# Layer 2 of chunks 8 to 23 by Strassen's seven products, with p multiplied into x ahead of layer 1

## Chip, cores and metric

One core of one Trainium2 chip. The metric is the device time of one execution, in microseconds (us), as a median over several runs. Every run that a comparison uses is fast (granted TensorE clock 0.994 to 1.0). The rounds ran on several chips, so kernels are compared by their ratio to the kernel before in the same rounds.

## The reference, cut

An RWKV-5 recurrence over 4 batches, 8 heads, 768 steps and 48 columns per head gives x (3072 rows of 384). A mixture of four dense experts, weighted by p, follows. This second part is where the change works:

```python
p = domain_probs / (domain_probs.sum(-1, keepdims=True) + 1e-09)
out = np.zeros((N, D))                    # N, D, E, F = 3072, 384, 4, 1024
for e in range(E):
    h = np.maximum(x @ w1[e], 0.0)        # layer 1
    out += p[:, e:e + 1] * (h @ w2[e])    # layer 2
```

## The kernel before: what the argument touches

The kernel works on 24 chunks of 128 rows; four chunks (one of each batch) make a superchunk, so there are six superchunks, 0 to 5. All matmuls are bf16. The attention of a chunk makes x; layer 1 takes a whole superchunk (512 columns), layer 2 one chunk at a time (8 matmuls of 384 columns for an expert), and p goes in as the layer-2 result leaves PSUM:

```python
def mm(ci=ci, s=s, i=None):                       # layer 2, one chunk, one expert
    ...
    for fb in range(NFB) ...:                     # NFB = 8
        nc.tensor.matmul(ps, tl["hTs", e, sc][:, fb, s, :], w2_sb[:, e, fb, :],
                         start=(fb == 0), stop=(fb == NFB - 1))

def evac(ci=ci):
    ...
    if e == 0:
        nc.scalar.mul(tl["oacc", ci], tl["o", e, ci], pe)
    else:
        nc.vector.scalar_tensor_tensor(tl["oacc", ci], in0=tl["o", e, ci], scalar=pe,
                                       in1=tl["oacc", ci], op0=ALU.mult, op1=ALU.add)
```

Attention gives VectorE, per chunk, two scales (RK), two masks (AtM), a row reduction (dcoef), one addition (Ysb) and the state update (Tn), and GpSimd the products ruk, dv and the other half of the state:

```python
eng.tensor_mul(RK[:, i, :, 0:D], tl[("Kt", "Rt")[1 - i], ci],
               tl["W", i] if ci < SUB and i not in on_pool else W_sd[i])      # scale, two inputs in SBUF
...
nc.gpsimd.tensor_mul(tl["ruk", ci], tl["Rt", ci], tl["Kt", ci])
...
nc.vector.tensor_mul(tl["AtM", ci][:, j], tl["At", ci, j], mask[...])         # the mask; At is in PSUM
...
nc.vector.tensor_add(tl["Ysb", ci]..., tl["Y", ci], tl["dv", ci])             # Ysb; Y is in PSUM
```

The order of instructions on each engine isn't written by hand. Every piece of work is a `job` with the engines that may do it and a duration in us, such as `{"V": 0.61}` for a mask on VectorE or `{"P": 0.98}` for ruk on GpSimd. When the program is built, a small planner plays these durations through and fixes the order and, where there is a choice, the engine. A wrong duration doesn't give a wrong result; it gives an order that doesn't fit. At run time each engine takes its instructions strictly in that order.

## Time and profile before

| | before |
|---|---|
| time, median of 3 runs (lowest to highest) | 295.73 us (294.98 to 295.81) |
| profiled span | 293.9 us |
| busy: PE, PEld, DVE, ACT, POOL | 287.9, 170.0, 159.4, 150.5, 105.5 us |

PE is TensorE's matmul, PEld its weight load (beside PE), DVE is VectorE, ACT ScalarE, POOL GpSimd. A window of the profile lists, for one stretch of the span, the busy time of each engine; 25.00 of 25.00 for PE means that TensorE had no gap. The prediction below shows the lines that matter; two further windows of the kernel before (columns: stretch, length, then PE, PEld, DVE, ACT, POOL busy with counts, granted clock, share of the transfer engines, GB/s):

```profile
75.00:100.00 25.00, 24.99 (x238) 15.74 (x236) 18.41 (x32) 12.12 (x21) 19.64 (x25) 1.00 0.79 152
150.00:175.00 25.00, 25.00 (x175) 13.76 (x174) 12.07 (x22) 12.39 (x22) 11.09 (x14) 1.00 0.61 131
```

TensorE is full, and VectorE is at 18.4 of 25 us early, at 12.1 later.

### The profile page before, as it was taken

How to read it: one execution, taken by the hardware profiler on the slowest of the kernel's cores; microseconds unless marked ns; L12 is line 12 of the kernel's file. 1: busy time of each engine (PE TensorE's matmuls, PEld its weight loads, DVE VectorE, ACT ScalarE, POOL GpSimd, SP SyncE). 2: the span in 40 equal slices, each digit the busy share in tenths (PEclk: the TensorE clock that was granted, in tenths of full speed). 3: DMA queues.
4: the chain of work that ended last, by engine and by line, in shares of the span. 5: the costliest groups of instructions: out<-in, count | busy, mean ns of one | idle time of the engine just before them, and what ended most of it. 6: DMA issues, size and time to landing. Idle time of an engine off the chain costs nothing.

```text
span 293.9 us, 5824 instructions
## 1 busy us (share of the span) xinstructions
PE 287.9 (98%) x2298; PEld 170.0 (58%) x2298; DVE 159.4 (54%) x300; ACT 150.5 (51%) x249; POOL 105.5 (36%) x138
## 2 busy tenths in 40 slices
PE   8989999999999999999999999999999999999995
PEld 3777566866855555555555555555555555555553
DVE  6877877786579895727537535546405222101223
ACT  4573968557843334464444464543564544565440
POOL 2885144844977583754522542411000000000000
PEclk9999999999999999999999999999999999999999
DMA  7999999999966769592192391130330100200003
GB/s 153 257 266 284 308 322 283 214 312 186 229 122 125 164 143 200 152 187 41 22 205 55 103 202 34 28 71 29 107 74 6 20 2 27 80 2 0 0 2 107
DMA packets 111199, 37.66 MB, mean 128 GB/s; under 512 B 99242, under 2 KB 111148, under 8 KB 111172
## 3 DMA queue, kind: packets, MB, share of 16 engines
q1 hardware_dynamic: 111156, 37.29, 53.7%
q8 instruction: 18, 0.29, 0.4%
q14 instruction: 9, 0.07, 0.1%
q10 hardware_dynamic: 16, 0.00, 0.0%
HBM read 26.79 MB, written 4.72 MB: 107 GB/s over the span
## 4 chain that ended last, share of the span: by engine, by line
PE 90%; SPq 6%; DMA 2%; POOL 0%; issue 0%; DVE 0%
PE out_ps L632 42%; PE hT_ps L602 37%; PE hT_ps L596 4%; SPq L191 4%; DMA wst<-in_moe_w_dram 2%; PE At_ps L436 2%; PE Y_ps L474 1%; SPq L205 1%; PE Y_ps L467 1%; PE St_ps L515 1%; SPq L202 1%; PE RKT_ps L394 1%; PE out_ps L565 0%; POOL w_sb L76 0%; PE xT_ps L500 0%
## 5 line engine op out<-in xcount | busy, mean ns | idle before, releaser
L613 ACT ACTIVATE hTs<-hT_ps 128x512 bf16<-128x512 f32 x168 | 99.8, 598 | 99.2 <-PE hT_ps L602 94.4
L632 PE MATMUL out_ps<-w_sb,hTs 128*128 128x384 bf16 x760 | 137.9, 326 | 0.1
L602 PE MATMUL hT_ps<-xTe,w_sb 128*128 128x512 bf16 x504 | 123.7, 379 | 0.0
L632 PEld LDWEIGHTS <-hTs 128*128 128x128 bf16 x760 | 72.9, 98 | 53.0 <-issue 0.2
L642 DVE SCALAR_TENSOR_TENSOR oacc<-out_ps,p_nat,oacc 128x384 f32<-128x384 f32 x71 | 43.6, 617 | 90.7 <-PE out_ps L632 89.5
L602 PEld LDWEIGHTS <-w_sb 128*128 128x128 bf16 x504 | 47.0, 98 | 46.4
L345 POOL TENSOR_TENSOR ruk<-Rt,Kt 128x384 f32<-128x384 f32 x24 | 23.9, 1000 | 43.3 <-DMA Kt<-in_k_dram 25.0
L445 DVE TENSOR_TENSOR AtM<-At_ps,mask 128x512 bf16<-128x512 f32 x48 | 30.7, 683 | 14.0 <-PE At_ps L436 14.0
L371 POOL TENSOR_TENSOR dv<-Vt,dcoef 128x384 f32<-128x384 f32 x24 | 21.3, 888 | 32.5 <-DVE Ysb L483 28.7
L353 POOL TENSOR_TENSOR ruk<-ruk,U_sd 128x384 f32<-128x384 f32 x23 | 24.7, 1075 | 0.9
L640 ACT ACTIVATE oacc<-out_ps,p_nat 128x384 f32<-128x384 f32 x24 | 13.8, 581 | 18.8 <-PE out_ps L632 14.7
L535 POOL TENSOR_TENSOR S<-Tn,wC 64x192 bf16<-64x192 f32 x32 | 17.3, 542 | 6.5 <-DVE Tn L530 5.0
L596 PE MATMUL hT_ps<-xTe,w_sb 128*128 128x128 bf16 x288 | 18.0, 219 | 0.9 <-ACT w_sb L72 0.7
L366 DVE TENSOR_REDUCE dcoef<-ruk 128x8 f32<-128x384 f32 x24 | 13.1, 545 | 10.7 <-POOL ruk L353 10.3
L76 POOL CAST Vb<-Vt 128x384 bf16<-128x384 f32 x20 | 12.4, 618 | 14.7 <-PE St_ps L515 6.8
L596 PEld LDWEIGHTS <-w_sb 128*128 128x128 bf16 x288 | 16.6, 98 | 1.5 <-ACT w_sb L72 0.9
L483 DVE TENSOR_TENSOR Ysb<-Y_ps,dv 128x384 bf16<-128x384 f32 x24 | 13.3, 553 | 6.6 <-PE Y_ps L474 5.2
L611 ACT ACTIVATE hTs<-hT_ps 128x512 bf16<-128x512 f32 x24 | 14.2, 597 | 4.3 <-PE hT_ps L596 3.3
L332 DVE TENSOR_TENSOR RK<-Kt,W_sd 128x384 bf16<-128x384 f32 x20 | 16.2, 814 | 0.0
L332 DVE TENSOR_TENSOR RK<-Rt,W_sd 128x384 bf16<-128x384 f32 x20 | 14.6, 734 | 0.2
L72 ACT CAST w_sb<-wst 128x768 bf16<-128x768 f32 (+1 forms) x12 | 11.9, 990 | 3.4 <-DMA wst<-in_moe_w_dram 3.3
L530 DVE TENSOR_TENSOR Tn<-S,St_ps 64x192 f32<-64x192 bf16 x32 | 11.1, 348 | 1.6 <-PE St_ps L515 0.9
(67 smaller groups left out, 138.1 us busy)
## 6 DMA issues: line engine op xcount, KB each, us to landing
wst<-in_moe_w_dram SPq DMA_DIRECT2D x16, 576.0 KB, 6.2
Kt<-in_k_dram SPq DMA_DIRECT2D x24, 192.0 KB, 3.9
Vt<-in_v_dram SPq DMA_DIRECT2D x24, 192.0 KB, 4.3
Rt<-in_r_dram SPq DMA_DIRECT2D x24, 192.0 KB, 3.7
out_dram<-oacc SPq DMA_DIRECT2D x23, 192.0 KB, 1.9
wst<-in_moe_w_dram SPq DMA_DIRECT2D x8, 384.0 KB, 6.7
RKT<-RK SPq DMA_TRANSPOSE x16, 3.2
xTe<-Ysb SPq DMA_TRANSPOSE x16, 2.3
```

The source lines that it names most:

```text
L332: eng.tensor_mul(RK[:, i, :, 0:D], tl[("Kt", "Rt")[1 - i], ci], tl["W", i] if ci < SUB and i not in on_pool else W_sd[i])
L345: nc.gpsimd.tensor_mul(tl["ruk", ci], tl["Rt", ci], tl["Kt", ci])
L353: nc.gpsimd.tensor_mul(tl["ruk", ci], tl["ruk", ci], U_sd)
L371: nc.gpsimd.tensor_mul(tl["dv", ci], tl["Vt", ci], tl["dcoef", ci].to_broadcast((128, H, D)))
L445: nc.vector.tensor_mul(tl["AtM", ci][:, j], tl["At", ci, j], mask[:, None, :].to_broadcast((128, NP, C)))
L535: nc.gpsimd.tensor_mul(S_new[pr, :, cl], tl["Tn", ci][pr], wC[pr, :, None].to_broadcast((P2, NP, D)))
L596: nc.tensor.matmul(ps[:, i, :], w1_sb[:, e, db, (fb + i) * 128:(fb + i + 1) * 128], xTe[:, db, s0, :], start=(i == 0 and db == 0), stop=(i ...
L602: nc.tensor.matmul(ps[:, 0:n, :].rearrange("p a b -> p (a b)"), w1_sb[:, e, db, fb * 128:(fb + 1) * 128], xTe[:, db, s0:s0 + n, :].rearran ...
L611: nc.scalar.activation(hTs[:, fb:fb + 4, s0, :], ps, AF.Relu)
L613: nc.scalar.activation(hTs[:, fb, s0:s0 + n, :], ps[:, 0:n, :], AF.Relu)
L632: nc.tensor.matmul(ps, tl["hTs", e, sc][:, fb, s, :], w2_sb[:, e, fb, :], start=(fb == 0), stop=(fb == NFB - 1))
L642: nc.vector.scalar_tensor_tensor(tl["oacc", ci], in0=tl["o", e, ci], scalar=pe, in1=tl["oacc", ci], op0=ALU.mult, op1=ALU.add)
```

## The change

Strassen's scheme forms a 2x2 block product from seven products instead of eight. Here the two row blocks are two chunks, the two column blocks halves of w2's 384 columns, and the inner blocks even and odd groups of the hidden dimension. Seven eighths of the matmul work of layer 2 remain, for additions on other engines. So that one scheme can run over all four experts as one long sum of products, p must already be inside the hidden values: x is multiplied by p (p is positive, so ReLU lets it through), once for each expert, before layer 1. The change does this for superchunks 2 to 5 (chunks 8 to 23). What each part costs:

- 20 weight mixes (sums of w2 blocks), once, on VectorE or GpSimd: `mix`;
- four scalings by p for each chunk, on ScalarE or VectorE, into one buffer `y_e`, which one transposing transfer of 12 blocks empties: `xs`;
- ten sums of hidden blocks for each pair of chunks, on VectorE: `sum`;
- seven products of 16 matmuls of 192 columns for each pair, and their combination into the output.

For room, buffers become fixed shared regions, some of them fewer (three input buffers for four, two of Ysb, ruk and dv for three). `GATES` says after which layer-1 group the attention of each pair of chunks may begin.

```diff
-    NIN = 4
+    NIN = 3
...
+    w2_t = weights.tile([128, 3, E, NFB // 2, Dm // 2], BF16)
+    hAll = weights.tile([128, E * NFB, SUB, 128], BF16)
+    NST = 12
+    stg = weights.tile([128, NST, 2 * Dm], F32)
...
+    GATES = (3, 3, 4, 2, 8, 10, 13, 19)
...
-    slots = dict(inp=NIN, wst=8, RKT=4, AtM=2, Ysb=3, ruk=3, dv=3, Vb=4, At=2, tr=1, ys=1,
-                 mm=4, xTe=3, hTs=3, oacc=12)
+    FIRST = 2                                        # first superchunk by Strassen
+    slots = dict(inp=NIN, RKT=3, AtM=2, Ysb=2, ruk=2, dv=2, Vb=4, At=2, tr=1, ys=1,
+                 mm=4, xTe=2, oacc=4, Yse=1)
...
+            def xs(e):
+                def run(eng):
+                    o = y_e[:, e * HD:(e + 1) * HD]
+                    if eng == "A":
+                        nc.scalar.mul(o, tl["Ysb", ci], p_nat[:, e, n_p:n_p + 1])
+                    else:
+                        nc.vector.tensor_scalar(o, tl["Ysb", ci], scalar1=p_nat[:, e, n_p:n_p + 1],
+                                                scalar2=None, op0=ALU.mult)
+                return run
+            for e in range(E):
+                job(("Xs", ci, e), {"A": 0.48, "V": 0.40}, xs(e), ...)
+            job(("Xout", ci), {"S": 1.3}, lambda: nc.sync.dma_start_transpose(
+                get_xTe(sc)[:, :, ci % B, :], y_e), ...)
...
+        def run(eng):                                # mix
+            (nc.vector if eng == "V" else nc.gpsimd).tensor_tensor(o, x, y, op=op)
+        job(("mix", e, what), {"V": 0.47, "P": 2.0}, run, needs, 14.0 + 0.1 * e)
...
+                    job(("sum", sc, q, m, hf), {"V": 0.62},
+                        lambda ...: nc.vector.tensor_tensor(S, a_of(*x, hf), a_of(*y, hf), op=op), ...)
...
+                    for n in range(8):               # one half of one product
+                        ...
+                        nc.tensor.matmul(tl["P", sc, q, m], st, moving(m, e, i),
+                                         start=(hf == 0 and n == 0), stop=(hf == 1 and n == 7))
```

The last chunk of before was split in two to shorten the end; the change drops that.

## The prediction

> **What bounds the kernel now.** I read the page first (busy shares, then the slices), then the sums by window, the chain, the groups, and last the timeline of the end and of one crowded stretch on VectorE and GpSimd.
>
> ```profile
> PE 287.9 (98%) x2298; PEld 170.0 (58%) x2298; DVE 159.4 (54%) x300; ACT 150.5 (51%) x249; POOL 105.5 (36%) x138
> ...
> PEclk9999999999999999999999999999999999999999
> ```
> ```profile
> 50.00:75.00 25.00, 25.00 (x283) 18.04 (x281) 19.53 (x33) 15.88 (x24) 14.92 (x18) 1.00 1.01 236
> 100.00:125.00 25.00, 25.00 (x201) 14.14 (x199) 18.95 (x35) 10.76 (x19) 15.35 (x20) 1.00 0.74 172
> 250.00:275.00 25.00, 25.00 (x137) 13.20 (x135) 3.45 (x6) 13.58 (x23) 0.00 (x0) 1.00 0.07 24
> ```
> The columns of the windows are length, then busy time of PE, PEld, DVE, ACT, POOL. From 25 us to the last store PE has no gap, at full clock. A busy matmul is not by itself a matmul at peak, so I check the pace:
> ```profile
> L632 PE MATMUL out_ps<-w_sb,hTs 128*128 128x384 bf16 x760 | 137.9, 326 | 0.1
> 252.49 1.30 PE out_ps L632 x8
> ...
> 253.79 1.94 PE hT_ps L602 x9
> ...
> 289.48 1.33 PE out_ps L565 x16
> ```
> The 326 ns is one matmul's latency; the chain gives the pace: 1.30/8 = 162.5 ns for 384 columns, 1.94/9 = 216 ns for 512, 1.33/16 = 83.1 ns for 192. So 760 + 504 matmuls of layers 2 and 1 are worth 123.5 + 108.9 us, the 288 small ones of layer 1 some 16 us (48 in 2.68 us), and the remaining 40 us or so are attention, its transposes, fillers and the wait at the start. The chain puts 42% of the span on L632 and 37% on L602. TensorE's amount of work is the bound; the first 25 us hang on loads, the last 3 us on an eviction and a store. VectorE is free on average but not early: 76% in 100 to 125 us, 14% in 250 to 275.
>
> **What the Trainium skill says.**
> 1. "TensorE: Matmul & The Clock Gate", Single matmul latency / Back-to-back issue gap: the isolated gap is N/2.4 + 2.5 ns, so 82.5 ns at 192 columns and 162.5 at 384. The trace agrees (83.1 and 162.5). The same section speaks of about 81 ns at N=128 where weights are reloaded each time; this trace does 55.8 ns there, so the measurement decides: weight loads don't bind at 83 ns.
> 2. "VectorE: DVE Perf Modes", Side-by-side: where the cycles go for N=2048 bf16: a 16-bit two-input add in SBUF runs two elements a cycle at most. The trace before has no such add; it shows two a cycle for a 16-bit copy (424 ns for 512 elements) and one a cycle for the f32 multiplies.
> 3. "SBUF — State Buffer", Who interferes with whom: a VectorE instruction with two SBUF inputs contends with a GpSimd one that reads SBUF, through an exclusive lock. The trace agrees: the scale multiply of K (L332) has minimum 545, median 856, maximum 1387 ns, and is long where GpSimd works:
> ```profile
> 88.20 1.35 DVE L332 TENSOR_TENSOR RK<-Kt,W_sd 128x384 bf16<-128x384 f32 x1
> ...
> 90.39 0.54 DVE L332 TENSOR_TENSOR RK<-Rt,W_sd 128x384 bf16<-128x384 f32 x1
> ```
> ```profile
> 87.81 1.32 POOL L353 TENSOR_TENSOR ruk<-ruk,U_sd 128x384 f32<-128x384 f32 x1
> ```
>
> **The change, part by part.**
> *TensorE.* Layer 2 of 16 chunks is now 504 matmuls of 384 columns and 16 of 192: 504 x 162.5 + 16 x 83.1 = 83.2 us. The instruction order of the changed kernel has 896 of 192 columns (8 pairs, 7 products, 16 matmuls): 896 x 83.1 = 74.5 us. Saved: 8.8 us; the ideal eighth (10.4) loses 1.6 to the fixed cost per matmul. Layer 1 stays at 504 + 288, attention is the same. The start has 96 fillers for 89: seven more at 56 to 110 ns, about +0.5 us of start.
>
> *Moved.* Layers 1 and 2 of a superchunk (four chunks) no longer mix: the order has 96 layer-1 matmuls (20.7 us), then 224 products (18.6 us), with attention between (0.82 us a chunk in the chain: 0.17 + 0.20 + 0.17 and half of a pair's 0.55; 3.3 us per superchunk): 42.6 us.
>
> *ScalarE.* In the pure layer-1 stretch one ReLU comes every 3 x 216 = 648 ns; back to back it takes 0.50 us (two in 1.10):
> ```profile
> 70.00 1.10 ACT L613 ACTIVATE hTs<-hT_ps 128x512 bf16<-128x512 f32 x2
> ```
> 32 x 0.50 = 16 of 20.7 us leave 4.7 us in each superchunk for the scalings by p that the order gives it (29 in all, about 7 x 0.5 = 3.6 us per superchunk). It fits, with four PSUM buffers.
>
> *VectorE.* Removed: 47 weighted accumulations of 617 ns, 29 us. Added: 80 sums of 128x1024 bf16, at two a cycle and the ~140 cycles that the 681 ns masks show over 512: (512 + 140)/0.96 = 0.68 us (estimate), 54 us; 48 combinations of 192 columns at (192 + 142)/0.96 = 0.35 us, 17 us; 8 wide ones at 0.55, 4; 35 scalings by p at about 0.4, 14; 11 weight mixes at about 0.55, 6. Net about +66 us: 159 becomes 225 busy. Successive instructions overlap by about 0.08 us (four masks in 2.48 us, not 2.72), which sets real capacity.
> One product group (two chunks): 10 x 0.60 + 6 x 0.27 + 0.47 = 8.1 us paced, 9.4 by durations, beside 112 x 83.1 = 9.3 us of PE. So pure product stretches (superchunks 4, 5) just go, with attention gone.
> Superchunks 2 and 3 carry attention too: 4 x 4.1 us paced (per chunk two scales 1.55, two masks 1.37, dcoef 0.55, Ysb 0.55, two Tn 0.70, less eight overlaps), p about 3.3, sums and combinations 16.2: 35.9 of 42.6 us, 84%. But scales average 0.77 for 0.545 alone, +0.23 from the lock; if the 20 sums and some 9 p scalings suffer likewise, +6.7: 42.6 us, 100%. This is the tight place.
>
> *GpSimd.* 9 mixes of about 2 us (twice 128x384's 1.0): +18 us before superchunk 2, in stretches where it is up to 79% busy. It also lengthens VectorE's locked time.
>
> *DMA.* Transposes of x carry four times the bytes. From 3 blocks in 2.3 us and 8 in 3.2, about 3.9 us for 12; with a single source buffer about 6 us a chunk, 24 of 43 us. Hidden. Weights come in 32 pieces for 24, same bytes.
>
> *Sum.* 295.7 - 8.8 + 0.5 = 287.4 with no new wait. I add 1.6: 0.2 us per product group (8) for sums arriving late through four buffers; each has 2.0 us (three halves of 8 matmuls) from the release of its buffer until use, of which two semaphore hops and the sum take some 1.1. **289.0 us.** I don't add the 100% in full, since the PE order already interleaves products with other pairs' where sums would be late.
>
> **The rivals.**
> 1. *Clean gain.* VectorE keeps up, nothing is lost: 286.5 to 287.5. For: before, this static order kept PE without a gap for 250 us with VectorE at 76%. Against: only 13% headroom within a product group, where sums form a chain with four buffers.
> 2. *VectorE with GpSimd's lock becomes the bound in superchunks 2 and 3.* PE takes its instructions in order, so a late mask or sum stops it: 3 to 4 us lost in each, 293 to 296, the gain nearly gone. For: the 100% above, and the extra 18 us of GpSimd. Against: superchunk 4's layer 1 has VectorE nearly empty, and PE order has no attention crowding in 4 and 5.
> 3. *The start or weights.* Three input buffers for four, with DMA at 1.01 in 50 to 75 us: late weights open gaps before 100 us, +1 to 3 us: 288 to 291. For: prefetch is shorter. Against: same bytes, and nearly the same loading order up to expert 1.
> 4. *The sums run one element a cycle* because each strides over blocks: 1.2 us each, product groups of 13 us against 9.3: about 315. Inner runs of 128 are contiguous, so I give it 3%.
>
> **Range and chances.** The 2% line is 289.8, only 0.8 above my number: up to 2.4 us of new waits still count as faster. Rival 1 and half of my own central case fall below it; rival 2 and part of 3 above. Faster 0.55, same 0.41, slower 0.04. Range 286.5 to 293.5: clean at the low end, most of rival 2 at the high one.
>
> **What would show it.** Matmul count 896 of 192 columns at 83 ns (1.33 us per 16) in the chain: the saving. PE busy 25.00 in all windows after 25 us: rival 1. Waits of PE's weight loads on VectorE's sums, of 0.1 to 0.3 us, about a product group each: my case. VectorE over 23 of 25 us in the middle windows, sums averaging 0.9 us there and 0.68 in the last two superchunks, and PE waiting for masks or sums by microseconds: rival 2. PE waits for casts before 100 us: rival 3. I am wrong in substance if new PE waits exceed 5 us or if time goes up.

## The result, and the profile after

| | before | after |
|---|---|---|
| time, median of 4 runs (lowest to highest) | 295.77 us (294.98 to 296.91) | 300.04 us (298.18 to 300.81) |
| profiled span | 293.9 us | 298.0 us |
| PE, DVE, ACT, POOL busy | 287.9, 159.4, 150.5, 105.5 us | 281.4, 230.0, 163.1, 125.9 us |

The ratio is 1.0131, with a 95% interval of 1.0092 to 1.0170: slower by 1.3%, within the 2% band, and above the predicted range. A ratio here comes from the fast runs of a kernel and of the kernel before in the same rounds, as the record gives it; it isn't quite the ratio of the quoted medians. Where I compare runs of different rounds below, I turn the ratio into us by (ratio - 1) x 295.7; the change is then +3.9 us.

The page of the changed kernel, busy times and slices (each digit a tenth of a slice of 7.45 us):

```profile
PE 281.4 (94%) x2660; PEld 192.3 (65%) x2681; DVE 230.0 (77%) x430; ACT 163.1 (55%) x285; POOL 125.9 (42%) x147
...
PE   8889999999979969999889999999999999999995
...
DVE  5877689899798999996999998979951179210685
```

PE fell from 98 to 94% of a longer span: TensorE has less to do and stands longer. Between the start and the last slice, the digits below 9 on PE lie in slices 12, 15, 20 and 21, which is about 82 to 156 us, and there VectorE stands at 9. (21 of the 2681 matmuls have no record, up to 2 us of apparent gaps.) The same in windows, columns as above:

```profile
50.00:75.00 25.00, 24.35 (x309) 18.43 (x306) 23.20 (x39) 15.35 (x25) 17.77 (x20) 1.00 0.95 241
75.00:100.00 25.00, 22.68 (x197) 13.32 (x198) 22.56 (x37) 13.49 (x23) 22.16 (x25) 1.00 0.97 170
100.00:125.00 25.00, 22.09 (x183) 12.69 (x185) 24.21 (x42) 9.92 (x18) 18.68 (x22) 1.00 0.90 167
125.00:150.00 25.00, 23.41 (x174) 11.67 (x176) 22.03 (x39) 18.48 (x34) 15.22 (x19) 1.00 1.05 202
150.00:175.00 25.00, 23.28 (x272) 20.32 (x271) 24.84 (x47) 7.45 (x15) 11.24 (x12) 1.00 0.78 149
225.00:250.00 25.00, 24.95 (x214) 18.52 (x215) 11.34 (x22) 13.61 (x24) 0.00 (x0) 1.00 0.08 23
```

From 50 to 175 us VectorE (third busy number) is at 22 to 25 of 25 us, where before it was at 12 to 19.5, and PE loses 0.7 to 2.9 us in each window. From 225 us on, with GpSimd at zero, PE is nearly full again.

The chain of work that ended last (start, duration, what) says what the gaps wait for. Stretches at 107, 134 and 160 us, and the product stretches of superchunks 4 and 5:

```profile
106.92 2.71 DVE stg L530 x3
109.63 0.48 DVE Ysb L514
110.11 0.04 issue
110.15 0.33 PE St_ps L562 x4
...
133.81 6.16 DMA stg<-stg
...
140.06 2.03 DVE stg L530 x3
142.09 0.48 DVE Ysb L514
142.57 0.04 issue
142.61 0.33 PE St_ps L562 x4
...
159.57 3.02 DVE stg L765 x4
...
237.01 18.61 PE M_ps L782 x224
...
276.34 18.62 PE M_ps L782 x224
```

L530 is the scaling by p on VectorE, L514 the Ysb of another chunk behind it in VectorE's order, L562 the state matmul of TensorE that can't begin until Y, which Ysb reads, has left PSUM. So three scalings, 2.71 us, hold up TensorE at 107 us; at 134 us a transposing transfer of the scaled x holds the scalings up first; at 160 us it's sums (L765). From 143 to 178 us the chain runs almost wholly on VectorE. In superchunks 4 and 5, by contrast, 224 products take 18.61 us: 83.1 ns each, without a gap.

The groups that the change added (busy us, mean ns of one, idle time before and its releaser):

```profile
L765 DVE TENSOR_TENSOR stg<-hAll 128x1024 bf16<-128x1024 bf16 x80 | 56.4, 737 | 41.3 <-ACT hAll L648 36.3
L530 DVE TENSOR_SCALAR stg<-Ysb,p_nat 128x384 bf16<-128x384 f32 x35 | 22.4, 686 | 1.9 <-DMA stg<-stg 1.7
L721 POOL TENSOR_TENSOR w_t<-w_sb 128x768 bf16<-128x768 bf16 x5 | 9.2, 1850 | 2.2 <-ACT w_sb L79 1.6 <-DVE w_sb L81 0.6
L721 DVE TENSOR_TENSOR w_t<-w_sb 128x768 bf16<-128x768 bf16 x7 | 7.4, 1073 | 1.4 <-POOL w_sb L83 1.2
L797 DVE TENSOR_TENSOR oacc<-oacc,M_ps 128x192 f32<-128x192 f32 x48 | 15.4, 348 | 1.8 <-PE M_ps L782 1.5
```

Sums average 737 ns (median 685, minimum 678), scalings 686 ns (406 to 1790), mixes on VectorE 1073. Such a spread for instructions of one size is what an instruction looks like that waits inside itself. The timeline (start, duration) of VectorE and then of GpSimd shows it happening:

```profile
102.22 1.34 DVE L362 TENSOR_TENSOR RK<-Rt,W_sd 128x384 bf16<-128x384 f32 x1
103.48 1.99 DVE L362 TENSOR_TENSOR RK<-Kt,W_sd 128x384 bf16<-128x384 f32 x1
```
```profile
102.15 1.00 POOL L375 TENSOR_TENSOR ruk<-Rt,Kt 128x384 f32<-128x384 f32 x1 [1.24 <-DMA Kt<-in_k_dram]
103.11 1.95 POOL L721 TENSOR_TENSOR w_sb<-w_sb 128x768 bf16<-128x768 bf16 x1
```

The scale alone takes 0.545 us. Behind GpSimd's ruk it takes 1.34 us, and behind a weight mix 1.99: it ends at 105.47, 0.41 us after the mix's end at 105.06. VectorE counts as busy all that time.

This holds throughout the trace. Of VectorE's scales, mixes, sums and scalings, 52 take over 50 ns longer than undisturbed, and every one ends a fixed time after the end of a GpSimd instruction: 0.41 to 0.42 us for scales and mixes, 0.55 for sums, 0.21 to 0.22 for scalings. So the scaling, with only one tensor as input, waits too. Counted as mean less minimum, times the number, this waiting fills 29 us of VectorE's time in the change (scalings 9.8, scales 9.5, mixes 5.3, sums 4.7), and 9 us, all in scales, before it.

**The arithmetic.** The matmul saving of 8.8 us and +3.9 us of time leave 12.7 us of lost time, where the prediction had 2.1: 1.6 of new waits and 0.5 at the start.

### The profile page after: what moved, and what is told of

It reads as the page before. It is cut to its first block, busy times and chain, and to the rows that moved or that the text cites. A ratio compares the mean times of both kernels' runs of the same rounds, so it can differ in the third digit from the quotient of the medians.

```text
span 298.0 us, 6749 instructions
## 1 busy us (share of the span) xinstructions
PE 281.4 (94%) x2660; PEld 192.3 (65%) x2681; DVE 230.0 (77%) x430; ACT 163.1 (55%) x285; POOL 125.9 (42%) x147
## 4 chain that ended last, share of the span: by engine, by line
PE 47%; DVE 12%; DMA 2%; issue 2%; DVEq 0%
PE hT_ps L637 23%; PE M_ps L782 19%; DVE stg L765 4%; PE out_ps L666 3%; DVE stg L530 2%; DMA stg<-stg 2%; DVE AtM L475 1%; DVE oacc L797 1%; DVE RK L362 1%; DVE Ysb L514 1%; PE At_ps L466 1%; DVE Tn L577 1%; PE St_ps L562 1%; PE Y_ps L504 0%; PE Y_ps L497 0%
## 5 line engine op out<-in xcount | busy, mean ns | idle before, releaser
L648 ACT ACTIVATE hAll<-hT_ps 128x512 bf16<-128x512 f32 x168 | 97.6, 598 | 43.1 <-PE hT_ps L637 34.7
L765 DVE TENSOR_TENSOR stg<-hAll 128x1024 bf16<-128x1024 bf16 x80 | 56.4, 737 | 41.3 <-ACT hAll L648 36.3
L637 PE MATMUL hT_ps<-stg,w_sb 128*128 128x512 bf16 x372 | 85.5, 379 | 0.6
L782 PEld LDWEIGHTS <-stg 128*128 128x128 bf16 x640 | 52.4, 98 | 2.3 <-DVE stg L765 1.9
L666 PE MATMUL out_ps<-w_sb,hAll 128*128 128x384 bf16 x256 | 46.7, 326 | 0.5 <-POOL w_sb L83 0.5
L782 PE MATMUL M_ps<-w_t,stg 128*128 128x192 bf16 x384 | 36.2, 246 | 0.4 <-DVE stg L765 0.4
L666 PEld LDWEIGHTS <-hAll 128*128 128x128 bf16 x256 | 23.8, 98 | 15.9 <-issue 0.9
L637 PE MATMUL hT_ps<-xTe,w_sb 128*128 128x512 bf16 x111 | 29.2, 379 | 0.6 <-DVE oacc L675 0.2
L782 PE MATMUL M_ps<-w_sb,stg 128*128 128x192 bf16 x256 | 24.4, 246 | 0.2 <-DVE stg L765 0.2
L530 DVE TENSOR_SCALAR stg<-Ysb,p_nat 128x384 bf16<-128x384 f32 x35 | 22.4, 686 | 1.9 <-DMA stg<-stg 1.7
L782 PE MATMUL M_ps<-w_sb,hAll 128*128 128x192 bf16 x256 | 23.1, 246 | 0.0
L782 PEld LDWEIGHTS <-hAll 128*128 128x128 bf16 x256 | 21.2, 98 | 0.6
L646 ACT ACTIVATE hAll<-hT_ps 128x512 bf16<-128x512 f32 x24 | 14.3, 601 | 8.0 <-PE hT_ps L631 7.4
```

The lines of the kernel that those rows point to most:

```text
L530: nc.vector.tensor_scalar(o, tl["Ysb", ci], scalar1=p_nat[:, e, n_p:n_p + 1], scalar2=None, op0=ALU.mult)
L637: nc.tensor.matmul(ps[:, 0:n, :].rearrange("p a b -> p (a b)"), w1_sb[:, e, db, fb * 128:(fb + 1) * 128], xTe[:, x0 + db, s0:s0 + n, :].re ...
L648: nc.scalar.activation(hTs[:, fb, s0:s0 + n, :], ps[:, 0:n, :], AF.Relu)
L666: nc.tensor.matmul(ps, relu_tile(e, sc)[:, fb, s, :], w2_sb[:, e, fb, :], start=(fb == 0), stop=(fb == NFB - 1))
L765: lambda S=S, x=x, y=y, op=op, hf=hf: nc.vector.tensor_tensor(S, a_of(*x, hf), a_of(*y, hf), op=op),
L782: nc.tensor.matmul(tl["P", sc, q, m], st, moving(m, e, i), start=(hf == 0 and n == 0), stop=(hf == 1 and n == 7))
```

## The experiments

The theory, called A in the expectations: new work on VectorE and on GpSimd makes VectorE late, partly because some instructions of the two exclude each other, and TensorE stands behind VectorE. A1 and A2 are two forms of its GpSimd part: exclusion by an instruction that reads, or merely the time that it takes in GpSimd's own queue. The rivals, under other letters or in words, lay the loss on what shorter VectorE and GpSimd instructions would not remove: fewer buffers, transfers, the weights, or the order as such.

All results in one table, fast runs alone. "us" is (ratio - 1) x 295.7.

| run | what it is | median us | ratio (95%) | us against before |
|---|---|---|---|---|
| the change | | 300.04 | 1.0131 (1.0092 to 1.0170) | +3.9 |
| e1_poolmix_short | GpSimd mixes a quarter as wide | 294.22 | 0.9976 (0.9917 to 1.0035) | -0.7 |
| e2_xs_short | VectorE scalings an eighth as wide | 295.45 | 1.0000 (0.996 to 1.004) | 0.0 |
| e3_sums_short | sums of superchunks 2, 3 an eighth as wide | 295.74 | 0.9993 (0.9966 to 1.0019) | -0.2 |
| e4_all_short | all three, and VectorE's mixes | 289.18 | 0.9769 (0.9740 to 0.9797) | -6.8 |
| e5_poolmix_memset | e1, GpSimd's time refilled by writes | 293.66 | 0.9943 (0.9923 to 0.9963) | -1.7 |
| f6_buffers_only | the change with no Strassen superchunk | 299.49 | 1.0138 (1.0113 to 1.0163) | +4.1 |
| g6_no_mixes | f6 without its mixes | 296.39 | 1.0028 (1.0014 to 1.0043) | +0.8 |
| f4_half | Strassen in superchunks 4, 5 | 294.88 | 0.9976 (0.9958 to 0.9994) | -0.7 |
| f3_after_order | Strassen in superchunks 3 to 5 | 294.07 | 0.9937 (0.9909 to 0.9964) | -1.9 |
| g3_early_gates | f3 with the change's early gates | 293.96 | 0.9915 (0.9883 to 0.9947) | -2.5 |
| g2_later_gates | the change with later gates | 297.98 | 1.0060 (1.0036 to 1.0084) | +1.8 |
| h1_two_sources | the change with two `y_e` buffers | 298.19 | 1.0054 (1.0024 to 1.0084) | +1.6 |
| b3_lock_aware | superchunks 3 to 5, order that knows the lock | 289.08 | 0.9782 (0.9768 to 0.9796) | -6.4 |
| b2_lock_aware_all | superchunks 2 to 5, order that knows the lock | 289.71 | 0.9813 (0.9782 to 0.9845) | -5.5 |

e1 to e5 keep every engine's instruction order and only shorten or refill instructions; their results are wrong. So that nothing reads an unwritten buffer, e1, e3, e4 and e5 also give the products other operands of the same size, and e2 and e4 add one memset of 1.38 us on GpSimd; the cuts below leave this out. All the others are correct.

**e1_poolmix_short.** The nine mixes on GpSimd touch a quarter of their columns.

```diff
-            (nc.vector if eng == "V" else nc.gpsimd).tensor_tensor(o, x, y, op=op)
+            n = 1 if eng == "P" else 4
+            (...).tensor_tensor(o[:, 0:n], x[:, 0:n], y[:, 0:n], op=op)
```

> The changed kernel with its instruction order kept, wrong result on purpose: the 9 weight mixes on GpSimd touch a quarter of their elements (about 0.5 us for 1.9), those on VectorE stay whole. The changed kernel takes 300.0 us. Theory A (VectorE is the bound between 64 and 172 us, its instructions with two SBUF inputs being locked out while GpSimd reads): some 12 us of GpSimd's lock time go, VectorE instructions in 64 to 132 us get shorter, 296 to 298 us. Theory B (fewer buffers and later loads open the gaps): no change, 299.5 to 300.5. Theory C (the single source buffer of the x transposes stalls VectorE's queue): no change.

Measured 294.22 us, 4.6 us below the change by ratios: more than I had expected of nine instructions. (The interval here is 1.7 us either way; e5, with the same cut and a narrow interval, is the surer number.) The window shows where; VectorE does as much per window as before, but PE hardly waits (22.09 in the change):

```profile
100.00:125.00 25.00, 24.82 (x188) 13.69 (x186) 24.11 (x47) 12.89 (x23) 18.84 (x25) 1.00 1.02 213
```

VectorE's own mixes fell from 1073 to 691 ns with nothing about them changed. They had been waiting for GpSimd's.

**e2_xs_short.** The 35 scalings by p on VectorE write 48 columns for 384.

```diff
-                        nc.vector.tensor_scalar(o, tl["Ysb", ci], ...
+                        nc.vector.tensor_scalar(o[:, 0:48], tl["Ysb", ci][:, 0:48], ...
```

> Order kept, wrong result: the 35 scalings of x by p on VectorE write 48 of 384 columns. They still wait for the transpose that frees their buffer. Theory A: about 15 us of VectorE work and lock waits go, of which a part was under slack: 295 to 297 us. Theory B: 299.5 to 300.5. Theory C: the waits for the transpose remain, 299 or more.

Measured 295.45, 3.9 us below the change. An eighth of the columns still took 490 ns on average (686 before): a scaling's time in this place lies mostly in something other than its columns. The shortest took 231 ns (406 before); the rest of the mean is waiting.

**e3_sums_short.** The 40 sums of superchunks 2 and 3 cover one block of eight.

```diff
-                            S, a_of(*x, hf), a_of(*y, hf), op=op),
+                            *((S, a_of(*x, hf), a_of(*y, hf)) if sc > 3 else
+                              (S[:, 0:1], a_of(*x, hf)[:, 0:1], a_of(*y, hf)[:, 0:1])), op=op),
```

> Order kept, wrong result: the 40 sums of superchunks 2 and 3 touch an eighth of their elements, those of 4 and 5 stay whole; TensorE does the same matmuls. Theory A: the some 6 us of TensorE waits between 139 and 189 us nearly vanish, those before stay: 294 to 296 us. Theory B: unchanged. Theory C: at most 1 us.

Measured 295.74, 4.1 us below. The gaps between 150 and 175 us, the products of superchunk 2, are gone (PE 23.28 in the change), while 75 to 125 us stays as in the change:

```profile
100.00:125.00 25.00, 22.69 (x188) 12.87 (x186) 24.15 (x44) 10.99 (x19) 19.13 (x24) 1.00 0.88 178
...
150.00:175.00 25.00, 25.00 (x290) 21.58 (x289) 20.00 (x51) 9.82 (x19) 10.98 (x14) 1.00 0.75 147
```

**e4_all_short.** All three edits, and VectorE's 11 mixes cut to a quarter too.

```diff
+            (...).tensor_tensor(o[:, 0:1], x[:, 0:1], y[:, 0:1], op=op)     # mix, on both engines
+                        nc.vector.tensor_scalar(o[:, 0:48], ...             # as e2
+                              (S[:, 0:1], a_of(*x, hf)[:, 0:1], ...         # as e3
```

> Order kept, wrong result: the three cuts together, with the mixes on VectorE cut to a quarter too. Theory A: nearly all of the 12.9 us of new TensorE waits go, 287 to 289.5 us, that is the time before less the 8.8 us of saved matmul time, plus one for the start. Theory B: 297 or more, since loads and buffers are as they were. Theory C: 297 or more.

Measured 289.18: 10.7 of the 12.7 us are back, with the same matmuls, buffers, transfers and order. So theory A holds for most of the loss, and what the rivals can have is some 2 us. This doesn't split the loss between the exclusion and the plain time of the added work. The single edits add up to 12.6 us, more than all together: they partly remove the same wait.

**e5_poolmix_memset.** As e1, but each short mix on GpSimd is followed by two memsets, which write but read nothing, so that GpSimd is as long occupied as in the change.

```diff
+            if eng == "P":
+                for k in range(FILL):                       # FILL = 2
+                    nc.gpsimd.memset(w2_t[:, what % 3, e, 1:4, :], 0.0)
```

> As the kernel with the nine GpSimd mixes cut to a quarter (which took 294.2 us), order kept, wrong result, but GpSimd then spends the time gained (1.4 us each) on two memsets that only write into parts of the mixed weights that nothing reads. Theory A1 (what hurts is that a GpSimd instruction which reads SBUF locks out VectorE): 294 to 295.5 us. Theory A2 (what hurts is the place that the mix takes in GpSimd's queue ahead of attention's products): 298.5 to 300.5 us. Between: both.

Measured 293.66, 5.6 us below the change and no worse than e1. The lines by form of this run show GpSimd's time refilled (0.61 to 0.81 us for the short mix and 2 x 580 ns, for 1.85 to 1.90), and VectorE's mixes still at 692 ns:

```profile
L726 POOL MEMSET w_t<- 128x576 bf16 x18 | 10.4, 580 | 1.0 <-DVE w_t L723 0.5
L723 DVE TENSOR_TENSOR w_t<-w_sb 128x768 bf16<-128x768 bf16 x7 | 4.8, 692 | 0.5 <-POOL w_sb L83 0.3
```

So it isn't GpSimd being late with its other work (A2): for instructions with two SBUF inputs, it's the reading instruction that shuts VectorE out (A1). The timelines of VectorE and GpSimd in this run show a limit of that. A mix ran undisturbed beside two memsets, but three scalings took 2.61 us, the last two ending 0.21 us after a memset each (1.21 and 0.81 us, for 0.41 undisturbed). Scalings wait behind writes as well, so e5 clears GpSimd's writes for mixes and scales alone.

```profile
79.62 0.54 DVE L723 TENSOR_TENSOR w_sb<-w_sb 128x768 bf16<-128x768 bf16 x1
...
101.32 2.61 DVE L531 TENSOR_SCALAR stg<-Ysb,p_nat 128x384 bf16<-128x384 f32 x3
```
```profile
79.52 1.21 POOL L726 MEMSET w_t<- 128x576 bf16 x2
...
102.41 1.30 POOL L726 MEMSET w_t<- 128x576 bf16 x2
```

**f6_buffers_only and g6_no_mixes.** `FIRST = 6` leaves no superchunk to Strassen: layer 2 as before, x transposed unscaled, but the new buffers, pieces, 20 unused mixes and the unsplit end, with gates by the rule of before. g6 is the same order without issuing the mixes.

```diff
-    FIRST = 2
+    FIRST = 6                                      # f6
...
+            if FIRST < NSC:                        # g6
                 (nc.vector if eng == "V" else nc.gpsimd).tensor_tensor(o, x, y, op=op)
```

> The changed program with Strassen for no chunk: all layer 2 is plain as before, p is applied at the eviction, but buffers, regions, weight pieces and loading order are those of the change; the attention gates follow the rule of before. Right result. If fewer buffers and shorter prefetch cost by themselves: 297 to 299 us. If they are free: 295.5 to 296.5. Theory B (loads and buffers make most of the loss) wants 300 or more.

> The run without Strassen (f6, 299.49 us) in the same instruction order, but its 20 weight mixes are not issued (9 on GpSimd, 11 on VectorE); correct result. It divides f6's 3.9 us over the kernel before. If the mixes' locked time in 50 to 100 us does it: 297 to 298. If the buffers, loads and the end that is no longer split do it: 299 to 300.

f6 takes 299.49, as slow as the change without any of its saving, between the two ranges expected. The label is misleading, because it isn't the buffers: g6 takes 296.39, below both of its ranges. The mixes cost 4.1 - 0.8 = 3.3 us, and buffers, pieces and the unsplit end 0.8 us in all (interval 0.4 to 1.3).

**f4_half and f3_after_order.** Strassen in the last two, and the last three, superchunks, with the change's table of durations (the gates had to follow).

```diff
-    GATES = (3, 3, 4, 2, 8, 10, 13, 19)
+    GATES = (3, 5, 7, 9, 11, 13, 15, 17)           # f4; f3: (3, 4, 6, 8, 10, 12, 14, 16)
-    FIRST = 2
+    FIRST = 4                                      # f4; f3: 3
```

> Strassen for chunks 16 to 23 alone, the rest of layer 2 plain, gates by the rule of before, planner constants unchanged. Right result. Half of the matmul saving, 4.4 us, and the sums fall in superchunks 4 and 5, where the changed kernel showed 224 products in 18.61 us without a gap; mixes are still spread early. Theory A: 293 to 296 us, depending on the mixes; theory B: that of the run with the buffers alone less about 4.

> Strassen on chunks 12 to 23 alone, as in b3 (289.08 us), but ordered with the change's own table of durations and its rules, without the lock. If b3's gain came from the order that knows of the lock: 292 to 296 (half-way between f4 at 294.88 less 2.2, and the change at 300.0). If it came from leaving out superchunk 2: 288.5 to 290.

Each superchunk saves 2.2 us of matmuls. From f6 to f4 the time falls by 4.8 us (4.4 saved: no loss); from f4 to f3 by 1.2 (2.2 saved, 1.0 lost); from f3 to the change it rises by 5.8 (2.2 saved, 8.0 lost). The intervals leave about 1 us of noise in each of these steps and 1.4 in the last, so the gain of 0.4 isn't clear of noise, the 1.0 hardly, and the 8.0 is. So the loss sits in superchunk 2: the list 0.8 + 3.3 - 0.4 + 1.0 + 8.0 makes the 12.7 us.

**g2_later_gates and g3_early_gates.** Is it superchunk 2's own work, or the early attention that its gates bring? One run gives the change f3-like gates, the other gives f3 the change's early ones.

```diff
+    GATES = (3, 4, 6, 8, 10, 12, 14, 17)           # g2, in the change
+    GATES = (3, 3, 4, 2, 10, 12, 14, 16)           # g3, in f3
```

> The change with one line altered: the gates, which say how early the attention of each pair of chunks may begin, are (3, 4, 6, 8, 10, 12, 14, 17) for (3, 3, 4, 2, 8, 10, 13, 19), so chunks 10 to 15 no longer come up to two experts early. Everything else is as in the change, with all 896 products; correct. If the 8 us between three and four Strassen superchunks come from attention pulled forward into 75 to 125 us: 293 to 296. If they come from the added work of superchunk 2 itself under an order that is blind to the lock: 298 to 301.

> The run with three Strassen superchunks in the change's own order (f3, 294.07 us) with the change's early gates for chunks 8 to 15 (3, 3, 4, 2). If early attention is what costs: 297 to 300. If it is superchunk 2's own sums and scalings: 293.5 to 295.5.

g2 is 2.1 us faster than the change (median 297.98, just under the second range expected), g3 no slower than f3. Early attention alone costs nothing; the gates cost about 2 us where superchunk 2's work falls into the same time. The bulk is that work itself.

**h1_two_sources.** The 6.16 us of transfer in the chain aren't an exclusion between engines. Here the scaled x goes into two buffers in turn, in the same order. (The operand of the filler matmuls at the start moves elsewhere to make room.)

```diff
-                    o = y_e[:, e * HD:(e + 1) * HD]
+                    if ("ye", ci) not in tl:
+                        tl["ye", ci] = (y_e, y_e2)[sum(k[0] == "ye" for k in tl) % 2]
+                    o = tl["ye", ci][:, e * HD:(e + 1) * HD]
```

> The change in its own order, with two source buffers in turn for the transposes of the scaled x (the second in free places beside the staging area; the spin operand moved into a free part of the hidden buffer for space). Correct. In the change the chain has one 6.16 us piece of such a transpose at 133.8 us, and three scalings on VectorE wait behind it. If the single source buffer is a cause beside the lock: 296 to 298.5. If the scalings only came late behind VectorE's other work and the lock is all: 299 to 301.

Measured 298.19, 2.3 us below the change; the two intervals just don't touch. Half of the gain lies where the wait was (PE 23.41 there in the change):

```profile
125.00:150.00 25.00, 24.64 (x198) 12.93 (x197) 23.53 (x40) 19.53 (x35) 15.89 (x19) 1.00 1.06 197
```

So the single source buffer is a second, smaller cause.

**b3_lock_aware and b2_lock_aware_all.** The planner learns what the traces show: a VectorE instruction of the kinds in `locks` and any GpSimd instruction wait for each other; durations are those measured without the wait. With it go smaller choices: casts of V off GpSimd (b3: all on ScalarE; b2: ScalarE or GpSimd), scalings by p on ScalarE alone (b3), dv of one chunk behind that of the chunk before, new gates and pads (margins that the planner leaves before a job of the attention). b3 runs Strassen in superchunks 3 to 5, b2 in 2 to 5 as the change does.

```diff
+    def locks(e, name):
+        if e == "P":
+            return True
+        return e == "V" and (name[0] in ("sum", "mix", "Xs", "cast") or
+                             name[0] == "scale" and name[1] >= SUB)
...
+        if locks(e, j.name):
+            us += max(0.0, lock["VP"[e == "V"]] - now)
+            lock[e] = now + us
...
-                job(("Xs", ci, e), {"A": 0.48, "V": 0.40}, xs(e), ...
+                job(("Xs", ci, e), {"A": 0.51}, xs(e), ...             # b3; b2: {"A": 0.51, "V": 0.34}
-        job(("mix", e, what), {"V": 0.47, "P": 2.0}, run, ...
+        job(("mix", e, what), {"V": 0.48, "P": 1.65}, run, ...
```

> A version meant to beat both: Strassen for chunks 12 to 23; the program's planner uses the measured durations and lets a VectorE instruction with two SBUF inputs and a GpSimd one wait for each other; p scaling and casts of V on ScalarE; gates chosen anew. Right result. Three quarters of the saving are 6.6 us; if theory A is all, and the planner now places waits rightly: 290 to 293 us. If it is not: 295 or more.

> All of chunks 8 to 23 by Strassen, as the change does, in the lock-aware order of b3 (gates for 16 chunks, p scalings on ScalarE or VectorE). Correct result. If the order was all that was wrong with the change: 286.5 to 289, at least 2 us below b3's 289.08 less nothing for superchunk 2. If superchunk 2 has more VectorE work than its time holds however it is ordered: 289.5 to 294.

b3 takes 289.08 us, b2 289.71. Both beat both kernels; b3 by 2.2% against before, with its whole interval beyond 2%; b2 by 1.9%, which leaves it unclear whether it passes 2%. b2 does the change's own work 9.4 us faster than the change. In b3 TensorE has no gap from 50 to 200 us; three of the windows:

```profile
75.00:100.00 25.00, 25.00 (x214) 14.35 (x212) 20.28 (x34) 13.78 (x26) 20.82 (x20) 1.00 0.71 141
100.00:125.00 25.00, 25.00 (x192) 14.09 (x191) 16.96 (x33) 15.85 (x31) 14.18 (x18) 1.00 0.95 203
150.00:175.00 25.00, 25.00 (x169) 13.19 (x168) 15.99 (x27) 17.98 (x33) 12.31 (x13) 1.00 0.67 139
```

VectorE fell to 16 to 20 of 25 us there. Against f3, the same amount of Strassen in the old order, b3 gains 4.5 us. I can't say how much of that is the order and how much the choice of engines; they were altered together. The waits didn't vanish: counted as above, they fill 22 us of VectorE's time in b2 and 19 in b3, for 29 in the change. The 7 us fewer in b2 are 5 in scalings (28 of them on VectorE for 35) and 2 in scales, while 14 casts of V left GpSimd; its mixes wait as long as before. b2 gains nothing over b3, though superchunk 2 saves another 2.2 us of matmuls: that superchunk just pays for itself here. By its expectation, 289.71 is the low end of the case in which superchunk 2 has more VectorE work than its time holds in any order; b2 doesn't rule that out.

## Why the prediction was wrong, by its own steps

It gave "faster" 0.55 and "same", which came, 0.41; by its own sign (new waits over 5 us, or the time going up) it is wrong in substance.

1. **The saving on TensorE: right.** 896 products at 83.1 ns, 224 in 18.61 us without a gap, and f4's 4.8 us for half of it (4.4 worked out).
2. **The start, +0.5 us: not settled.** PE is 21.80 us busy in the first 25, for 22.27 before; but in e1 to e5 and h1, which keep the change's order, it lies anywhere from 21.10 to 23.10.
3. **Durations on VectorE: half right.** Sums 0.68 predicted, 0.685 median; combinations 0.35 and 0.348. Scalings by p, 0.40, and mixes on VectorE, 0.55, are right for undisturbed ones (least 0.406 and 0.546), but the waits make the means 0.69 (10 us in all) and 1.03 (5 us). Total DVE busy is 230 against 225, so the sum was nearly right, and it wasn't where the prediction failed.
4. **"This is the tight place" (superchunks 2 and 3 alone): wrong in its limits.** The prediction's balance of 35.9 of 42.6 us began at superchunk 2's layer 1. That layer 1 starts at 125 us in the trace; the mixes run from 26 us and the scalings from 88, and VectorE is at 22 to 24 of 25 us from 50 us on. e1, which only touches the mixes, gave its gain between 75 and 125 us, and f6 lost 3.3 us to mixes with no Strassen at all. Superchunk 3 lost 1.0 us, superchunk 2 lost 8.0.
5. **GpSimd's mixes: right length, no cost.** "About 2 us" each was right (1.85 to 1.90). That they lengthen VectorE's locked time stood there as a remark without a number. It was worth 3.3 us in f6 against g6, and 4.6 to 5.6 us in the change (e1, e5).
6. **"Hidden" for the transposes from one source buffer: wrong.** It compared a chunk's 6 us with 43 us available, but chunks of a superchunk come bunched: one such transfer stands with 6.16 us on the chain, and a second buffer is worth 2.3 us.
7. **The failed step: adding 1.6 us and not "the 100% in full, since the PE order already interleaves products with other pairs' where sums would be late".** An order protects against lateness only as far as its table of durations is true, and this one has 0.40 us for a scaling that takes 0.69 with its waits, 0.47 for a mix that takes 1.03, and no exclusion at all. The lost time came to 12.7 us. An order that had the exclusion, with other engine choices and otherwise much the same durations (0.34 for a scaling, 0.48 for a mix, 0.61 for a sum), cut it, with the same work, to about 3.3 (b2: 8.8 saved, 5.5 gained).
8. **The rivals.** Rival 2 named the mechanism, and its sign in the profile (VectorE over 23 of 25 us, PE waiting by microseconds) came true in 100 to 125 and 150 to 175 us. Its sums of 0.9 us came out at 0.82 for superchunk 2 (20 in 16.37 us of VectorE time) and 0.69 for superchunk 3 (20 in 13.87). It was too small at 293 to 296, because it counted only superchunks 2 and 3, and it got too little weight. Rival 3's reduced buffers cost, with the pieces and the unsplit end, 0.8 us in the order without Strassen (g6); in the change e4 leaves some 2 us for them and all else. Rivals 1 and 4 are refuted by the gaps and by 0.685 us a sum.

What stays open: how superchunk 2's 8.0 us divide between its sums, scalings and attention, and how much of them is exclusion and how much plain work. The single edits overlap (e2 3.9, e3 4.1, e1 4.6 us, together 10.7), so they bound the parts but don't split them.

## What to carry to other kernels

Before trading matmuls for additions, ask which engine's instructions will shut each other out, and add up the exclusive time of VectorE and GpSimd together in each stretch, not the busy share of each. A fixed order made from a table of durations is only as good as the table: after a change that adds instructions, put the undisturbed durations and the exclusion into the planner before judging the idea, because here the same work took 300.0 us in one order and 289.7 in another, with some of it on other engines. And a spread of durations among instructions of one shape (0.406 to 1.79 us for one scaling) can be a wait that the profile books as busy time, as it was here: look whether the long ones end together with an instruction of another engine.

## What the Trainium skill lacked or had wrong

- "SBUF — State Buffer", Who interferes with whom: its rule that a VectorE instruction with two SBUF inputs is shut out by a GpSimd instruction that reads SBUF, not by one that only writes, is borne out (scale 0.545 us alone, 1.99 behind a mix; in e5 a mix of 0.54 us beside memsets). It lacks a sense of size: nine reading GpSimd instructions of 1.9 us were worth 4.6 us of this kernel's time.
- "TensorE: Matmul & The Clock Gate", Back-to-back issue gap: the sustained figures for streams that reload weights each time, about 81 ns at N=128 and 131 at N=512, don't fit the traces read here: with a weight load for every matmul the chain shows 55.8 ns at 128 columns (48 in 2.68 us), 83.1 at 192 and 216 at 512 (1.94 us for 9).
- No page says how to plan an instruction order around this exclusion, beyond one line of advice in "SBUF — State Buffer" (to schedule whichever of the two is off the critical path); here it was worth 9.4 us of 300 (the change against b2, engine choices included).
